# Staging x's seven units in PSUM at the joints of pairs, in a Strassen-type attention and mixture-of-experts kernel on one core

## The chip, the core and the metric

The kernel runs on one core of one Trainium2 chip. The metric is device time in microseconds. The engines are named as in the profile: PE (matmul), PEld (its weight loads), DVE (vector), ACT (scalar), POOL (GpSimd), SP (the queue that issues DMAs). Each engine works through its own instructions in program order, and engines wait for each other by semaphores.

## The reference

```python
# attention in chunks of 64 tokens: q, k, v are (8, 8, 576, 64)
scores = scale * np.matmul(q_c, k_c.transpose(0, 1, 2, 4, 3))
attn = np.exp(scores - max) / (sum + 1e-09)
out = np.matmul(attn, v_c)
# the result as x (4608, 512) goes through 4 experts, w1 (4, 512, 1024), w2 (4, 1024, 512)
p = domain_probs / (domain_probs.sum(-1, keepdims=True) + 1e-09)
for e in range(E):
    h = np.maximum(x @ w1[e], 0.0)
    out += p[:, e:e + 1] * (h @ w2[e])
```

## The kernel before

The 4608 tokens are nine blocks of 512. The first block is done plainly; the other eight are four pairs (0 to 3) of two blocks. For a pair the kernel makes eight passes, one for each half of each expert (passes 8 to 39 of the program), so the last passes of a pair that another one follows are 15, 23 and 31. The stretch from such a pass into the next is called a joint here; joints 1, 2 and 3 lie around 475 to 531, 796 to 852 and 1113 to 1169 us of the profile.

A pass multiplies matrices of 2 by 2 blocks with seven products instead of eight (Strassen's scheme). Every float32 operand is split into a high part (rounded to the type that PE multiplies, by a cast on ACT) and a low part (what the rounding left, a subtraction on DVE or POOL), and a product is six matmuls of 128x512, three for each of two blocks of rows. For x of a pair the seven units are `b11 b21 b22 t1 t2 t3 t4`; their parts lie in tiles `xh0..xh6` and `xl0..xl6`. They stay the same through the pair's eight passes and have to be made anew at a joint, while PE still works on the old ones.

The order of PE is written out in `WOVEN`, 28 steps to a pass: `g` and `h` are products of x with w1 (the two column groups), `a` and `b` are products of the pass before with w2.

```python
WOVEN = (
    "a1 g1 a2 g2 g6 a5 g5 a6 a3 g7 a7 g4 g3 a4 h1 h2 b1 b5 h6 b6 b3 h5 b7 h7 b2 b4 h4 h3".split()
)
```

Behind each step `later_pass` issues the work of the other engines that is listed for it in `at`; the number in `add(at, 13, ...)` is the step's place in `WOVEN` from 0. So a step's number sets the place of the work in each engine's order. `late` is the list that goes into the following pass. A step of that following pass is written with a stroke here: a1', g1', a2' are its first three.

The names in the profile's rows: `A`, `B`, `C` are PSUM banks of PE's sums. `s<-A` (L711, ACT) keeps the running sum of a product, and the next x product waits for it. `wraw<-A,s` or `wf<-C,ws` (L811, DVE) are the hidden values; `hf` are their high parts (L823, ACT) and low parts (L826, POOL); `wraw<-wf,wraw` (L817, DVE or POOL) are sums of hidden values. `acc<-A,acc` (L873, DVE) adds an output product to its sum, after which PE may write that bank again. L363 and L366 are the helpers that make a high and a low part. In pass 15 and 16 alone `wf<-v_in`, `wf<-e` and the like (L503 on ACT, L504 on POOL) also make the last factors of w2.

`psa` is one PSUM tile of two banks, `[128, 2, 512]`, in which the attention's scores live. In the last pass of a pair no attention runs, and there the kernel of before puts the unit t4 in it. `e` and `pt` are the attention's two SBUF tiles, which there hold the unit t2.

Of the kernel before, what the change touches and what calls it, by code (L numbers as in the profile page):

```python
# [12 lines left out]
ALU = mybir.AluOpType  # L13
# [18 lines left out]
def chunk_attention_moe(ctx: ExitStack, tc: tile.TileContext, qk, v, v0, dp, w1, w2, out):  # L32
# [10 lines left out]
    nc = tc.nc  # L43
# [72 lines left out]
    psa = ps_a.tile([P, 2, 2 * HG * C], F32, name="psa")  # L116

    def a_load(t):
        s = st[t] = {}
        s["x"] = load.tile([P, 2, 2, HG, C], F32, name="qk_in")  # L120
        nc.sync.dma_start(out=s["x"], in_=qk[t].rearrange("g c d x h s -> (c d) g x h s"))
# [240 lines left out]
    def hi_part(src, t):  # L362
        nc.scalar.copy(out=t[0], in_=src)  # L363

    def lo_part(eng, src, t):
        eng.tensor_tensor(out=t[1], in0=src, in1=t[0].bitcast(F32), op=ALU.subtract)  # L366
# [203 lines left out]
    xt = {}  # L570
# [11 lines left out]
    class Tokens:  # L582
# [26 lines left out]
            for k, t in enumerate(self.t2):  # L609
                eng.tensor_tensor(out=t, in0=self.b22[:, k], in1=self.t1[:, k], op=ALU.subtract)  # L610

        def sum4_apart(self):

            for k, t in enumerate(self.t2):
                nc.vector.tensor_tensor(out=psa[:, k], in0=self.b21[:, k], in1=t, op=ALU.subtract)
            self.t4 = psa

        def split2(self):
            i = self.KEYS["t2"]
            x_alloc(i)  # L620
            for k, t in enumerate(self.t2):
                hi_part(t, [part[:, k] for part in xt[i]])

        def lo2(self, k):
            lo_part(nc.vector, self.t2[k], [part[:, k] for part in xt[self.KEYS["t2"]]])

        def sum3(self, eng=None):
            self.less("t3", "b22", "b12", self.b12, eng)
# [220 lines left out]
    class Outer:  # L849
# [17 lines left out]
        def add(self, src, i, s):  # L867
            key = self.n // n_pass, 2 * i + self.g + NK * s
            if key not in acc:
                acc[key] = opool.tile([P, SUB], F32, name=f"acc{key[1]}")  # L870
                nc.scalar.copy(out=acc[key], in_=src)
            else:
                nc.vector.tensor_tensor(out=acc[key], in0=src, in1=acc[key], op=ALU.add)  # L873
# [493 lines left out]
    def probs_load(n, s):  # L1367
        e = n % n_pass // 2
        i = int(s == 0 and e % 2)
        if i:  # L1370
            pb[1:] = [hpool.tile([P, SUB], F32, name="s4")]
        elif not pb:
            pb.append(wpool.tile([P, PAIR, SUB], F32, name="ws"))
        t = pb[1] if i else pb[0][:, s]
        r = e * n_tiles + (1 + (n // n_pass - 1) * PAIR + s) * NT
        nc.sync.dma_start(
            out=t, in_=p_t[r : r + NT, :].rearrange("t p -> (t p)").partition_broadcast(P)
        )
# [14 lines left out]
    def first_load(pair):  # L1393
        if pair < n_pairs:
            a_load((1 + pair * PAIR) * NT)
# [69 lines left out]
    def half_sums(at, g, places, eng=None):  # L1465
        for i, name in zip(places, SUMS):
            if i is not None:
                add(at, i, lambda name=name: half_sum(g, name, eng))
# [3 lines left out]
    def later_pass(n, ahead, late, held):  # L1472

        first_pass, last_pass = n % n_pass == 0, n % n_pass == n_pass - 1
        pair, more = n // n_pass - 1, n + 1 < n_run
        at, first = {}, {}
        left, sc = Units(n), Scaled(n)
        steps = {"gh"[g]: LaterGroup(g, left, sc, False) for g in range(2)}
        steps |= {"ab"[g]: Outer(g, n - 1, ahead[1], ahead[0], False) for g in range(2)}

        def put(i, name, k, of=sc):
            add(at, i, lambda: of.hi(name, k), lambda: of.lo(name, k))

        for f in held:
            add(at, 0, f)
        second_half(at, ahead[0], *((9, False) if n == n_pass + 1 else ()))
        for i, f in late:
            add(at, i, f)

        add(at, 12, lambda: sc.sum("t3", 0, nc.gpsimd))  # L1490
        put(16, "b11", 0)
        put(16, "b11", 1)
        add(at, 18, lambda: sc.sum("t2", 0))
        put(19, "t2", 0)
        put(20, "b22", 0)
        add(at, 22, lambda: sc.sum("t1", 0))
        put(22, "t3", 0)
        put(23, "t1", 0)
        put(24, "b21", 0)
        put(24, "b22", 1)  # L1500
        put(26, "b21", 1)
        if more:
            add(at, 26, lambda: sc.sum("t4", 0, nc.gpsimd))
        add(at, 27, lambda: sc.sum("t1", 1), lambda: sc.sum("t3", 1))
        for i, f in later:
            add(at, i - len(WOVEN), f)
        later.clear()
        if n % 2 and more:
            add(at, 18, lambda: probs_load(n + 1, 0))
            add(at, 27, lambda: probs_load(n + 1, 1))  # L1510
        if pair + 1 < n_pairs:
            for places, i in TILES.get(n % n_pass, ()):
                attend(at, pair + 1, (16, 20, 23) if pair == 0 and places == LATE else places, i)
        late = []
        if n + 1 < 2 * n_pass - 1:
            add(at, 5, lambda: half_load(n + 1, 0))
            add(at, 13, lambda: half_load(n + 1, 1, (0,)))
            add(at, 19, lambda: half_load(n + 1, 1, (1,)))
            half_sums(at, 0, (12 if n % n_pass in (3, 5) else 15, 21, 21, 21))
        if n_pass < n < 2 * n_pass - 1:  # L1520
            half_sums(first, 1, (5, 6, 9, 10) if n == n_pass + 1 else (8, 8, 8, 12))
            if n == n_pass + 1:
                half_sums(first, 0, (None, None, None, 3))
            for i in (3, 10, 12, *MAKE_AT[3:]) if n == n_pass + 1 else MAKE_AT:
                add(first if i == 24 else at, i, lambda: make_next(0))
        for m, makes, raws in (
            (2 * n_pass - 1, (20, 26), ((8, load, "v_in"), (21, load, "v_in"), (22, att, "e"), (23, att, "pt"))),
            (2 * n_pass, (4, 9, 11, 14, 20), ((1, hpool, "s4"), (2, load, "v_in"), (13, hpool, "s4"))),
        ):
            if n == m:  # L1530
                for i in makes:
                    add(at, i, lambda: make_next(1))
                    add(at, i + 2, keep_made) if i + 2 < len(WOVEN) else later.append((i + 2, keep_made))
                for i, *place in raws:
                    add(at, i, lambda place=place: raw_load(*place))
        if n == 2 * n_pass - 1:
            add(at, 0, x_back)
        if first_pass and pair > 0:
            for i in range(4):
                for after, f in enumerate(outputs(pair - 1, 2 * (i // 2), i % 2)):  # L1540
                    add(at, 15 + 3 * i + after, f)
            apart = 4 if pair == 1 else 3
            late = [
                (1 + apart * i + after, f) for i in range(4)
                for after, f in enumerate(outputs(pair - 1, 1 + 2 * (i // 2), i % 2))
            ]
        if last_pass and more:
            xs = []

            def x(what, *args):  # L1550
                return lambda: getattr(xs[0], what)(*args)

            add(at, 5, lambda: xs.append(Tokens(pair + 1)), x("sum1"))
            add(at, 8, x("sum3", nc.gpsimd), x("sum2_apart", nc.gpsimd))
            add(at, 13, x("sum4_apart"))
            add(at, 15, x("hi", "b11"))
            add(at, 16, x("hi", "b21"), x("lo", "b11"))
            add(at, 18, x("lo", "b21"))
            add(at, 20, x("split2"), x("lo2", 0))
            add(at, 22 if pair == 0 else 20, x("lo2", 1))  # L1560
            add(at, 23, x("hi", "t1"))
            add(at, 25 if pair == 0 else 24, x("lo", "t1"))
            add(at, 25, x("hi", "t3"))
            add(at, 26, x("hi", "t4"))
            late = [
                (0, x("hi", "b22")), (0, lambda: first_load(pair + 2)), (5 if pair == 0 else 1, x("lo", "t3")),
                (6, x("lo", "t4")), (8, x("lo", "b22")),
            ]
        for i, name in enumerate(WOVEN):
            getattr(steps[name[0]], f"p{name[1]}")()  # L1570
            for f in first.get(i, []) + at.get(i, []):
                f()
        return (sc, left), late, ()

    def second_half(at, sc, t4=6, sum4=True):

        add(at, 0, lambda: sc.sum("t2", 1))
        add(at, 1, lambda: sc.hi("t1", 1), lambda: sc.lo("t1", 1))
        add(at, 3, lambda: sc.hi("t2", 1), lambda: sc.lo("t2", 1))
        add(at, 4, lambda: sc.hi("t3", 1), lambda: sc.lo("t3", 1))  # L1580
        if sum4:
            add(at, 4, lambda: sc.sum("t4", 1, nc.gpsimd))
        for k in range(2):
            add(at, t4 + k, lambda k=k: sc.hi("t4", k), lambda k=k: sc.lo("t4", k))
# [125 lines left out]
```

## Time and profile before

| what | us |
|---|---|
| three runs, median (lowest to highest) | 1485.78 (1485.12 to 1486.92) |
| span of the profiled execution, first to last instruction | 1484.2 |
| PE busy | 1467.3, 99% |
| PEld, DVE, POOL, ACT busy | 1201.5, 1086.1, 975.1, 625.3 (81, 73, 66, 42%) |

The profiled execution's own time is given as its span alone; the median of the runs is 1.6 us above it, which lies around the span. PE is busy all through: the other engines matter where PE has to wait for them. The clock that PE was granted is 0.998 of full speed, so its upper level, 2.4 GHz, all along.

### The profile page before, as it was taken

Reading aid. Unit: us, or ns where it says so; the run is one execution under the profiler, and the core shown is the slowest. Engines: PE = TensorE matmul, PEld = TensorE weight load, DVE = VectorE, ACT = ScalarE, POOL = GpSimd, SP = SyncE. Lnnn points to the kernel's source line nnn. Section 1 sums busy time; section 2 is a strip of 40 time slices with the busy share of each in tenths; the row PEclk is TensorE's granted clock in tenths of the full one; section 3 lists DMA queues with packets and bytes.
Section 4 is the critical chain, followed back from the end, with each engine's and each line's share of the span. In section 5 each row is a group of like instructions: output and inputs, shape, how many; then the busy total and the mean of one; then the engine's idle time right before and its main releaser. Section 6 shows DMA issues by size and latency. Waiting matters only on the chain.

```text
span 1484.2 us, 23314 instructions
## 1 busy us (share of the span) xinstructions
PE 1467.3 (99%) x8556; PEld 1201.5 (81%) x8556; DVE 1086.1 (73%) x1492; ACT 625.3 (42%) x1165; POOL 975.1 (66%) x728
## 2 busy tenths in 40 slices
PE   8999999999999999999999999999999999999998
PEld 7888887888888778888888888888888888888887
DVE  5566667899897876777776977777778866666665
ACT  4556534545453434334343434343433333333332
POOL 5778887888877785455557665545557655555555
PEclk9999999999999999999999999999999999999999
DMA  8799785878777679666665688666665696665655
GB/s 306 268 329 338 282 323 195 272 232 272 238 262 239 233 239 283 221 211 226 201 221 196 218 212 276 203 230 213 216 200 201 198 257 195 202 206 193 206 192 147
DMA packets 199074, 346.94 MB, mean 234 GB/s; under 512 B 70048, under 2 KB 110256, under 8 KB 198576
## 3 DMA queue, kind: packets, MB, share of 16 engines
q1 hardware_dynamic: 198960, 345.45, 71.0%
q8 instruction: 68, 1.11, 0.3%
q14 instruction: 46, 0.38, 0.1%
HBM read 274.01 MB, written 71.38 MB: 233 GB/s over the span
## 4 chain that ended last, share of the span: by engine, by line
PE 88%; POOL 5%; DMA 3%; DVE 2%; issue 1%; ACT 1%; SPq 1%; POOLq 0%; DVEq 0%; ACTq 0%
PE A L648 46%; PE C L648 26%; PE B L648 13%; POOL hf L826 2%; PE psa L208 1%; POOL wf L504 1%; PE psa L161 1%; DMA wf<-in_w 1%; POOL hf L366 1%; DMA v_in<-in_v 1%; POOL wraw L817 0%; DMA wf<-w 0%; DVE xl L366 0%; POOL wf L366 0%; DVE acc L873 0%
## 5 line engine op out<-in xcount | busy, mean ns | idle before, releaser
L826 POOL TENSOR_TENSOR hf<-wraw,hf 128x512 fp32r<-128x512 f32 x384 | 504.1, 1329 | 228.5 <-ACT hf L823 223.2
L648 PE MATMUL A<-hf,wf 128*128 128x512 f32 x1536 | 392.3, 391 | 0.3 <-POOL hf L826 0.2
L648 PE MATMUL A<-xh,wf 128*128 128x512 f32 (+1 forms) x1104 | 380.9, 388 | 1.2 <-DVE wraw L811 1.2
L823 ACT CAST hf<-wraw 128x512 fp32r<-128x512 f32 x384 | 234.4, 622 | 283.0 <-DVE wraw L817 88.5
L648 PEld LDWEIGHTS A<-hf,wf 128*128 128x128 f32 x1536 | 287.4, 188 | 63.4 <-DVE acc L873 3.1
L648 PEld LDWEIGHTS A<-xh,wf 128*128 128x128 f32 x1104 | 206.7, 188 | 44.5 <-DVE wraw L811 1.6
L711 ACT COPY s<-A 128x512 f32<-128x512 f32 x192 | 112.9, 588 | 305.7 <-PE A L648 305.6
L648 PE MATMUL A<-xl,wf 128*128 128x512 f32 (+1 forms) x552 | 213.7, 388 | 0.0
L648 PE MATMUL C<-xh,wf 128*128 128x512 f32 (+1 forms) x600 | 205.5, 390 | 3.0 <-POOL wf L504 2.2
L873 DVE TENSOR_TENSOR acc<-A,acc 128x512 f32<-128x512 f32 x232 | 158.0, 682 | 66.1 <-PE A L648 65.0
L648 PE MATMUL C<-hf,wf 128*128 128x512 f32 x768 | 195.6, 390 | 2.6 <-POOL wf L504 2.0
L648 PEld LDWEIGHTS C<-hf,wf 128*128 128x128 f32 x768 | 143.8, 188 | 33.8 <-POOL wf L504 2.4
L817 POOL TENSOR_TENSOR wf<-wraw,wf 128x512 f32<-128x512 f32 x31 | 40.6, 1310 | 150.2 <-DVE wf L811 150.2
L648 PEld LDWEIGHTS C<-xh,wf 128*128 128x128 f32 x600 | 111.5, 188 | 27.7 <-POOL wf L504 2.6
L648 PE MATMUL B<-xh,wf 128*128 128x512 f32 (+1 forms) x376 | 125.2, 384 | 0.0
L873 DVE TENSOR_TENSOR acc<-C,acc 128x512 f32<-128x512 f32 x120 | 82.7, 689 | 53.8 <-PE C L648 52.8
L648 PEld LDWEIGHTS A<-xl,wf 128*128 128x128 f32 x552 | 103.5, 188 | 21.1
L826 POOL TENSOR_TENSOR hf<-wf,hf 128x512 fp32r<-128x512 f32 x64 | 94.0, 1469 | 33.9 <-ACT hf L823 33.5
L648 PE MATMUL C<-xl,wf 128*128 128x512 f32 (+1 forms) x300 | 114.9, 386 | 0.0
L817 DVE TENSOR_TENSOR wraw<-wf,wraw 128x512 f32<-128x512 f32 x64 | 95.3, 1489 | 5.2 <-POOL hf L826 4.1
L648 PE MATMUL B<-hf,wf 128*128 128x512 f32 x384 | 98.4, 391 | 0.5 <-POOL hf L826 0.5
L817 POOL TENSOR_TENSOR wraw<-wraw 128x512 f32<-128x512 f32 x63 | 92.1, 1462 | 0.0
(199 smaller groups left out, 1957.2 us busy)
## 6 DMA issues: line engine op xcount, KB each, us to landing
wf<-w SPq DMA_DIRECT2D x399, 512.0 KB, 4.2
w<-wf SPq DMA_DIRECT2D x49, 512.0 KB, 5.1
qk_in<-in_qk SPq DMA_DIRECT2D x32, 512.0 KB, 5.0
w<-hf SPq DMA_DIRECT2D x28, 512.0 KB, 7.5
w<-hf SPq DMA_DIRECT2D x42, 256.0 KB, 5.5
wf<-in_w SPq DMA_DIRECT2D x19, 512.0 KB, 7.0
ws<-p_t SPq DMA_DIRECT2D x24, 256.0 KB, 3.9
xraw<-in_w SPq DMA_DIRECT2D x24, 256.0 KB, 5.2
```

The lines of the kernel that those rows point to most:

```text
L161: nc.tensor.matmul(s["sc"][of_half(half), c, slot], lhsT=q, rhs=k, start=True, stop=True)
L208: nc.tensor.matmul(av[of_half(slot % 2), half, head // 2], lhsT=s["v"][of_half(half), head], rhs=s["pt"][of_half(half), c, slot], start=Tr ...
L366: eng.tensor_tensor(out=t[1], in0=src, in1=t[0].bitcast(F32), op=ALU.subtract)
L504: nc.gpsimd.tensor_tensor(out=t[:, :, 1], in0=src, in1=t[:, :, 0].bitcast(F32), op=ALU.subtract)
L648: nc.tensor.matmul(out, lhsT=lhs(k, a), rhs=rhs(k, b), start=first and i == 0, stop=last and i == len(parts) - 1, skip_group_check=not (fi ...
L711: nc.scalar.copy(out=t, in_=self.a)
L817: (eng or nc.vector).tensor_tensor(out=self.values[place, k], in0=self.values[a, k], in1=self.values[b, k], op=op)
L823: nc.scalar.copy(out=self.part(name, 0)[:, k], in_=self.values[name, k])
L826: (eng or nc.gpsimd).tensor_tensor(out=self.part(name, 1)[:, k], in0=self.values[name, k], in1=self.part(name, 0)[:, k].bitcast(F32), op=A ...
L873: nc.vector.tensor_tensor(out=acc[key], in0=src, in1=acc[key], op=ALU.add)
```

## The change

Before, DVE took a unit's low part from where the unit lies in SBUF, in one subtraction of 128x1024 (two of 128x512 for t2). Now ACT first copies the unit, in two halves of 128x512, to `psa` (`stage`), and DVE subtracts from there, half by half (`lo_staged`). t4 is now computed in place in SBUF from the staged t2 (`sum4_staged`) instead of into `psa`; and the steps at which the parts are made are others.

```diff
-        def sum4_apart(self):
-
-            for k, t in enumerate(self.t2):
-                nc.vector.tensor_tensor(out=psa[:, k], in0=self.b21[:, k], in1=t, op=ALU.subtract)
-            self.t4 = psa
+        def stage(self, name):
+
+            of = getattr(self, name)
+            for k in range(2):
+                nc.scalar.copy(out=psa[:, k], in_=of[k] if name == "t2" else of[:, k])
+
+        def lo_staged(self, name):
+            for k in range(2):
+                lo_part(nc.vector, psa[:, k], [part[:, k] for part in xt[self.KEYS[name]]])
+
+        def sum4_staged(self):
+
+            for k in range(2):
+                nc.vector.tensor_tensor(
+                    out=self.b21[:, k], in0=self.b21[:, k], in1=psa[:, k], op=ALU.subtract
+                )
+            self.t4 = self.b21
...
-            add(at, 13, x("sum4_apart"))
-            add(at, 15, x("hi", "b11"))
-            add(at, 16, x("hi", "b21"), x("lo", "b11"))
-            add(at, 18, x("lo", "b21"))
-            add(at, 20, x("split2"), x("lo2", 0))
-            add(at, 22 if pair == 0 else 20, x("lo2", 1))
-            add(at, 23, x("hi", "t1"))
-            add(at, 25 if pair == 0 else 24, x("lo", "t1"))
-            add(at, 25, x("hi", "t3"))
-            add(at, 26, x("hi", "t4"))
+            add(at, 14, x("stage", "b11"))
+            add(at, 15, x("hi", "b11"), x("lo_staged", "b11"))
+            add(at, 16, x("hi", "b21"))
+            add(at, 17, x("stage", "b21"))
+            add(at, 18, x("lo_staged", "b21"))
+            add(at, 19, x("stage", "t2"))
+            add(at, 20, x("split2"), x("lo_staged", "t2"), x("sum4_staged"))
+            add(at, 22, x("stage", "t1"))
+            add(at, 23, x("hi", "t1"), x("lo_staged", "t1"))
+            add(at, 24, x("stage", "t3"))
+            add(at, 25, x("hi", "t3"), x("lo_staged", "t3"))
+            add(at, 26, x("hi", "t4"), x("stage", "t4"))
             late = [
-                (0, x("hi", "b22")), (0, lambda: first_load(pair + 2)), (5 if pair == 0 else 1, x("lo", "t3")),
-                (6, x("lo", "t4")), (8, x("lo", "b22")),
+                (0, x("hi", "b22")), (0, x("lo_staged", "t4")), (0, lambda: first_load(pair + 2)),
+                (1, x("stage", "b22")), (2, x("lo_staged", "b22")),
             ]
```

PE's, POOL's and SP's instructions stand in the same order as before. ACT's and DVE's do not. First ACT at joint 2, from the keeping of h6's sum (`s<-A`) to the cast of t3's high part; `xh_8339` of before and `xh_8365` of now are t2's high part, `qk_in` holds t1. Before:

```order
L711 COPY s_8312<-A_8255 128x512
L823 CAST hf_8326<-wraw 128x512
L823 CAST hf_8336<-wraw 128x512
L363 CAST xh_8339<-e 128x512
L363 CAST xh_8339<-pt 128x512
L823 CAST hf_8362<-wf_8243 128x512
L711 COPY s_8374<-A_8255 128x512
L823 CAST hf_8379<-wraw 128x512
L363 CAST xh_8382<-qk_in 128x1024
```

The same place now, where each stage waits for DVE to have read the unit before it out of `psa`:

```order
L616 COPY psa<-xraw 128x512 x2
L720 COPY s_8335<-A_8273 128x512
L832 CAST hf_8350<-wraw 128x512
L616 COPY psa<-e 128x512
L616 COPY psa<-pt 128x512
L832 CAST hf_8362<-wraw 128x512
L363 CAST xh_8365<-e 128x512
L363 CAST xh_8365<-pt 128x512
L832 CAST hf_8390<-wf_8263 128x512
L616 COPY psa<-qk_in 128x512 x2
L720 COPY s_8404<-A_8273 128x512
L832 CAST hf_8409<-wraw 128x512
```

Six copies have come in between; the keeping of h7's sum (`s_8404`) now stands behind t1's two copies.

DVE at joint 2, from the hidden values of h7 to those of h4 (`wraw<-A,s`), for which g1' waits. Before:

```order
L811 SCALAR_TENSOR_TENSOR wraw<-B_8373,ws 128x512
L873 TENSOR_TENSOR acc_6031<-B_8385,acc_6031 128x512
L366 TENSOR_TENSOR xl_8383<-qk_in,xh_8382 128x1024
L873 TENSOR_TENSOR acc_6193<-A_8279,acc_6193 128x512
L811 SCALAR_TENSOR_TENSOR wraw<-A_8255,s_7619 128x512
```

Now:

```order
L820 SCALAR_TENSOR_TENSOR wraw<-B_8403,ws 128x512
L366 TENSOR_TENSOR xl_8413<-psa,xh_8412 128x512 x2
L882 TENSOR_TENSOR acc_6051<-B_8417,acc_6051 128x512
L882 TENSOR_TENSOR acc_6213<-A_8301,acc_6213 128x512
L366 TENSOR_TENSOR xl_8442<-psa,xh_8441 128x512 x2
L820 SCALAR_TENSOR_TENSOR wraw<-A_8273,s_7639 128x512
```

The low part of t3 (`xl_8442`), which stood in the next pass, now stands ahead of the hidden values of h4.

DVE in the first steps of the pass behind joint 2, from the sum at a1' to the sum at a5' (`acc<-C`), for which a3' waits. Before:

```order
L873 TENSOR_TENSOR acc_5817<-A_8438,acc_5817 128x512
L817 TENSOR_TENSOR wraw<-wraw 128x512
L366 TENSOR_TENSOR xl_8409<-xraw,xh_8408 128x1024
L873 TENSOR_TENSOR acc_5817<-B_8464,acc_5817 128x512
L846 TENSOR_TENSOR B_8474<-B_8474,s_8459 128x512
L811 SCALAR_TENSOR_TENSOR wraw<-B_8474,ws 128x512
L873 TENSOR_TENSOR acc_5879<-C_8499,acc_5879 128x512
```

Now:

```order
L882 TENSOR_TENSOR acc_5837<-A_8475,acc_5837 128x512
L826 TENSOR_TENSOR wraw<-wraw 128x512
L366 TENSOR_TENSOR xl_8458<-psa,xh_8457 128x512 x2
L882 TENSOR_TENSOR acc_5837<-B_8504,acc_5837 128x512
L366 TENSOR_TENSOR xl_8485<-psa,xh_8484 128x512 x2
L855 TENSOR_TENSOR B_8516<-B_8516,s_8498 128x512
L820 SCALAR_TENSOR_TENSOR wraw<-B_8516,ws 128x512
L882 TENSOR_TENSOR acc_5899<-C_8541,acc_5899 128x512
```

Two low parts (t4, b22) stand ahead of that sum instead of one (t3), the second behind a stage of ACT.

## Rows read from the trace of the kernel before

**Rows 1.** The waits of PE over the whole span: who waited for whom, us in total, times, longest.

```profile
PE C L648 <- POOL wf L504: 4.2, 2, 2.2
...
PE A L648 <- DVE wraw L811: 1.2, 1, 1.2
```

**Rows 2.** Busy time of each engine at the three joints (us and instructions), the granted clock, the DMA engines' share and GB/s.

```profile
474.00:531.00 57.00, 53.32 (x232) 42.80 (x231) 49.13 (x56) 24.41 (x39) 46.36 (x33) 1.00 0.71 246
796.00:852.00 56.00, 56.00 (x247) 45.93 (x246) 50.16 (x60) 23.45 (x37) 41.78 (x29) 1.00 0.63 206
1113.00:1169.00 56.00, 56.00 (x247) 45.91 (x246) 50.18 (x60) 23.45 (x37) 41.87 (x29) 1.00 0.59 197
```

**Rows 3.** PE in order of time at joint 1: start, us, what, and in brackets the idle time before and what ended it. The first is g1', the second within a5', the third within a3'.

```profile
516.59 0.50 PE L648 MATMUL A<-xh,wf 128*128 128x512 f32 x1 [1.18 <-DVE wraw L811]
...
523.72 0.73 PE L648 MATMUL C<-hf,wf 128*128 128x512 f32 x2 [0.48 <-POOL hf L826]
...
529.66 1.20 PE L648 MATMUL C<-hf,wf 128*128 128x512 f32 x4 [2.02 <-POOL wf L504]
```

**Rows 4.** DVE in order of time at joint 1: t1's low part and the hidden values of h4.

```profile
513.62 2.31 DVE L366 TENSOR_TENSOR xl<-qk_in,xh 128x1024 fp32r<-128x1024 f32 x1
515.86 0.68 DVE L811 SCALAR_TENSOR_TENSOR wraw<-A,s 128x512 f32<-128x512 f32 x1
```

**Rows 5.** POOL in order of time at joint 1, beside these.

```profile
510.59 4.27 POOL L826 TENSOR_TENSOR hf<-wraw,hf 128x512 fp32r<-128x512 f32 x3
```

**Rows 6.** The low parts by their inputs (line L366, DVE): ns at least, median, at most; first and last start in us; shapes.

```profile
L366 DVE TENSOR_TENSOR xl<-xraw,xh x17: 1211/1651/2340, 179.3 to 1165.4; 128x1024 fp32r<-128x1024 f32 x17
...
L366 DVE TENSOR_TENSOR xl<-B,xh x3: 676/692/692, 13.3 to 29.2; 128x512 fp32r<-128x512 f32 x3
...
L366 DVE TENSOR_TENSOR xl<-psa,xh x3: 1212/1215/1215, 527.2 to 1162.8; 128x1024 fp32r<-128x1024 f32 x3
```

**Rows 7.** ACT's operations by form: count, busy us, mean ns of one, idle time before them. PSUM to SBUF, SBUF to SBUF, PSUM to PSUM, and the cast of a whole unit.

```profile
L823 ACT CAST hf<-wraw 128x512 fp32r<-128x512 f32 x384 | 234.4, 622 | 283.0 <-DVE wraw L817 88.5 <-POOL wraw L817 69.0 <-PE A L648 53.5
L711 ACT COPY s<-A 128x512 f32<-128x512 f32 x192 | 112.9, 588 | 305.7 <-PE A L648 305.6
...
L243 ACT ACTIVATE psa<-psa 128x512 f32<-128x512 f32 x33 | 19.3, 585 | 77.7 <-DVE psa L240 73.5 <-DVE xraw L491 4.0
L363 ACT CAST xh<-xraw 128x1024 fp32r<-128x1024 f32 x18 | 18.8, 1051 | 4.5 <-PE B L648 2.3 <-DVE xraw L595 2.2
```

**Rows 8.** ACT in order of time where the attention places its weights: L198 writes the tile that L194 wrote, and waits for it.

```profile
450.36 0.59 ACT L711 COPY s<-A 128x512 f32<-128x512 f32 x1 [1.69 <-PE A L648]
450.85 0.59 ACT L194 COPY pt<-psa 128x512 f32<-128x512 f32 x1
451.47 1.49 ACT L198 COPY pt<-psa 32x256 f32<-32x256 f32 x4
```

**Rows 9.** PE in order of time at joint 2: the last two matmuls of b6, the whole of b7, the last of h7, then b4, a1', the first matmul of g1', and a3'.

```profile
823.60 0.62 PE L648 MATMUL A<-hf,wf 128*128 128x512 f32 x2
...
826.77 1.65 PE L648 MATMUL A<-hf,wf 128*128 128x512 f32 x6
...
829.41 0.39 PE L648 MATMUL A<-xh,wf 128*128 128x512 f32 x1
...
831.00 1.52 PE L648 MATMUL A<-hf,wf 128*128 128x512 f32 x6
...
835.16 1.66 PE L648 MATMUL A<-hf,wf 128*128 128x512 f32 x6
836.65 0.39 PE L648 MATMUL A<-xh,wf 128*128 128x512 f32 x1
...
846.17 1.52 PE L648 MATMUL C<-hf,wf 128*128 128x512 f32 x6
```

**Rows 10.** DVE in order of time at joint 2.

```profile
823.21 1.77 DVE L817 TENSOR_TENSOR wraw<-wf,wraw 128x512 f32<-128x512 f32 x1 [0.58 <-POOL hf L826]
...
830.21 1.18 DVE L817 TENSOR_TENSOR wraw<-wraw 128x512 f32<-128x512 f32 x1
...
832.03 0.69 DVE L811 SCALAR_TENSOR_TENSOR wraw<-B,ws 128x512 f32<-128x512 f32 x1
...
834.42 0.68 DVE L873 TENSOR_TENSOR acc<-A,acc 128x512 f32<-128x512 f32 x1
835.03 0.68 DVE L811 SCALAR_TENSOR_TENSOR wraw<-A,s 128x512 f32<-128x512 f32 x1
...
845.10 0.68 DVE L873 TENSOR_TENSOR acc<-C,acc 128x512 f32<-128x512 f32 x1
```

**Rows 11.** ACT in order of time at joint 2: b21's high part, then the keeping of h7's sum, the cast of the hidden values' t1, and the high part of x's t1.

```profile
821.22 1.05 ACT L363 CAST xh<-xraw 128x1024 fp32r<-128x1024 f32 x1
...
829.90 0.59 ACT L711 COPY s<-A 128x512 f32<-128x512 f32 x1 [0.74 <-PE A L648]
831.42 0.62 ACT L823 CAST hf<-wraw 128x512 fp32r<-128x512 f32 x1 [0.94 <-DVE wraw L817]
831.94 1.04 ACT L363 CAST xh<-qk_in 128x1024 fp32r<-128x1024 f32 x1
```

**Rows 12.** POOL in order of time at joint 2.

```profile
820.87 3.56 POOL L826 TENSOR_TENSOR hf<-wraw,hf 128x512 fp32r<-128x512 f32 x2 [3.27 <-ACT hf L823]
...
832.12 1.30 POOL L826 TENSOR_TENSOR hf<-wraw,hf 128x512 fp32r<-128x512 f32 x1 [1.28 <-ACT hf L823]
```

More of the change, by code (lines that the diff above doesn't have):

```diff
@@ L622, in split2 @@
                 hi_part(t, [part[:, k] for part in xt[i]])
-        def lo2(self, k):
-            lo_part(nc.vector, self.t2[k], [part[:, k] for part in xt[self.KEYS["t2"]]])
         def sum3(self, eng=None):
```

## The prediction

> **What bounds the kernel now.** I read the busy times first: PE is busy for 99% of the span, so time can be won or lost only where PE waits. The view of PE's waits comes next [rows 1]: the longest are for POOL making factors (L504) and for DVE's hidden values (L811). Then the three joints by themselves [rows 2]: PE stands for 57.00 - 53.32 = 3.68 us at joint 1 and not at all at joints 2 and 3, where it is busy for 56.00 of 56.00 us. The clock is at its upper level in all three, so nothing is to be had there. The timeline of joint 1 says where the 3.68 us lie [rows 3]: 1.18 ahead of g1', 0.48 within a5', 2.02 within a3'.
>
> The first of them shows what the change is about. t1's low part took 2.31 us [rows 4], against 1.21 for the fastest of such [rows 6]. POOL's three operations beside it ended at 510.59 + 4.27 = 514.86 [rows 5], and the subtraction ended 1.07 later, at 515.93: it had stood until POOL was through. POOL is held in the same way: two operations take 3.56 us at joint 2 [rows 12] where one alone takes 1.30. When DVE has a PSUM input no such holding shows: from a bank the subtraction takes 676 to 692 ns, from `psa` 1212 to 1215 [rows 6].
>
> So the change can win at most 3.68 us, all at joint 1. What it can lose is open, as DVE and ACT stand right behind PE: at joint 2 DVE's `acc<-A` ends at 834.42 + 0.68 = 835.10 and a1' starts at 835.16; the hidden values of h4 end at 835.71, and g1' starts at 836.65 [rows 9, 10], a margin of 0.94.
>
> **What the change costs, in busy time.** A unit's low part becomes two subtractions of about 0.69 that start 0.60 apart, so about 1.29 from start to end against 1.21 unheld: nothing to speak of for DVE. ACT gets 14 copies more at a joint. None from SBUF to PSUM stands in the trace; the nearest rows are 622 ns SBUF to SBUF, 588 PSUM to SBUF and 585 PSUM to PSUM [rows 7], so I take 0.59. The second half writes the same tile as the first and waits for it. Such a wait costs 0.03: 450.85 + 0.59 = 451.44, and the next starts at 451.47 [rows 8]. A stage is then 2 x 0.59 + 0.03, about 1.22. Bounds: 1.07 if the halves overlap as 450.36 and 450.85 do (0.49 apart), 1.27 at 0.62 each. 7 x 1.22 is 8.5 us more of ACT, which is busy for 24 of 57 us there [rows 2]: no bound by itself.
>
> The Trainium skill's page "ScalarE: Activation LUTs", section "Step-by-step: what each stage is for", says that ScalarE writes PSUM faster than SBUF. In the rows the two differ by 3 ns (585 and 588), so by them nothing changes; were a copy 0.1 us shorter by that rule, each joint's loss below would be some 0.8 us less.
>
> **What it costs in order.** `psa` holds one unit. A stage may start only when DVE has read the unit before, and DVE may subtract only when stage and high part are done; both engines take their work in order, so each of these waits also holds what stands behind it. Joint 2 worked through, with the orders of ACT and DVE shown above. An operation's successor on its engine starts 0.08 to 0.10 before its end; hand-overs are 0.03 between ACT and DVE (831.39 to 831.42) [rows 10, 11] and 0.10 from PE to ACT (829.80 to 829.90) [rows 9, 11].
> - POOL's two operations at 820.87 are no longer held and end at 823.41 (1.25 + 1.29). DVE's sum behind them, now done at 823.21 + 1.77 = 824.98, is done 0.55 later, at 823.96 (the same 0.55 as now: 820.87 + 3.56 = 824.43). This is the gain, 1.0 us.
> - b21 has been staged by then (822.17 to 823.39). Its low part: 823.88 to 825.16.
> - ACT stages t2: 825.19 to 826.41, then casts a hidden value and t2's high part (0.52 + 0.52 + 0.62): 827.97. DVE: t2's low part from 827.48, t4 in place to 829.96. DVE's next sum ends at 830.56, and b4 needs it at 831.00: just in time.
> - ACT stages t1: 829.99 to 831.21. Behind it stand the keeping of h7's sum, a cast and t1's high part: 833.18 (before: 831.94 + 1.04 = 832.98, with nothing behind it waiting).
> - DVE: t1's low part 833.21 to 834.49, then two sums, the second done at 835.69. a1' starts at 835.74, not 835.16.
> - ACT stages t3: 834.52 to 835.74, its high part ends at 836.69. DVE: t3's low part 836.72 to 838.00, then the hidden values of h4, done at 838.60. g1' starts at 838.65 and not at 836.65: **2.0 us lost**.
>
> Behind that, DVE makes h3's hidden values (to 839.93) and three sums, the first two each held by POOL: 841.16 and 842.9. For the third, DVE is ready at 843.42, and POOL's next operation can start at 843.36, too near to call. If POOL is first the sum is done at 845.2, else at 844.0; call that S. Then come t4's low part (1.20), b22's stage, which waits for it (0.03 + 1.22), b22's low part (0.03 + 1.28), two operations on g2' (0.72 + 0.61 less the overlap of 0.08) and `acc<-C` (0.68): S + 5.7, where it is done at 845.10 + 0.68 = 845.78 now. a3' needs it. Unhindered, a3' would start seven products of 1.36 behind g1', at 848.2; it starts at 849.7 or 850.9 instead of 846.17 [rows 9]: 3.55 or 4.75 lost. I take the middle, **4.15 us**, and the same at joint 3, whose rows agree with joint 2's [rows 2].
>
> Joint 1 by the same walk: a cast more (L503) stands ahead of t2's high part and moves the chain by 0.52, so h4's hidden values end at 517.80 and g1' starts at 517.85 instead of 516.59. Then ACT's cast of the hidden values' t2 stands behind b22's stage and ends at 526.8; POOL's four operations from there (4 x 1.27, no longer held) end at 531.9, and the third matmul of a3' starts at 531.98, not 529.66 [rows 3]: **2.3 us lost** although POOL is free of DVE.
>
> The sum: 2.3 + 2 x 4.15 = 10.6 us. The median lies 1.6 above the span of the profiled execution (1485.78 and 1484.2); nothing there changes, so 1485.8 + 10.6 = **1496.4**. With stages of 1.07 instead of 1.22, four of which lie on each chain, it is 1.8 less (1494.6); with 1.27, 0.6 more. A dozen hand-overs and the two ties leave some 4 us to either side: the likeliest case by itself runs from 1490 to 1500.
>
> **Rivals.** *Relief (faster).* DVE and POOL no longer hold each other, the stalls of joint 1 go, and nothing new comes: 1485.8 - 3.7 = 1482.1. For it speaks every held row above; against it, that the same rows give 1.0 us at joint 2 and the chain takes 3.0. It decides if the hidden values of h4 are done by 836.6 at joint 2, that is if three stages cost some 2 us less than I say. The Trainium skill states the holding as a rule ("GPSIMD Engine Reference", section "Key points": its SBUF interfaces are shared with VectorE, with contention from instructions with two SBUF inputs), and rows 4 and 5 agree with it; the rule is silent on ACT, where I see the cost.
>
> *Absorbed (no change).* The margins (0.94 at g1') and the relief at joint 1 (up to 3.7) pay for most of it: a loss of 1 us at each of joints 2 and 3 and a gain of 1 to 2 at joint 1 come to about 1486. It needs a chain 1 us shorter at each joint and DVE first in the ties.
>
> **How the numbers follow.** 0.2% is 3 us, and about what a measurement of this kernel can tell from no change. Slower by the chain: 0.78. Absorbed: 0.11. Relief: 0.11, counted as faster by over 0.2%. The range from 1486.5 to 1500 leaves out relief, a small part of the second case (0.04) and the end of the first above 1500 (0.04).
>
> **What would show it.** Right: PE waits at joints 2 and 3, ahead of g1' for DVE's L820, some 1.5 to 2.5 us, and within a6' and a3' for ACT, POOL or DVE; ACT idle ahead of its stages (L616), ended by DVE's L366; POOL's operations there near 1.3 instead of up to 1.8; low parts from `psa` at 0.69. Wrong: copies to PSUM well below 0.5 or the halves running into each other; low parts that start before their stage's second half; or joints 2 and 3 without a wait of PE, whatever the total.

## The result and the profile after

The changed kernel takes **1500.07 us** (1499.63 to 1501.63), the kernel before 1486.24 (1485.12 to 1486.92) on the same chip: a ratio of 1.0095, 95% interval 1.0084 to 1.0107. That is 13.8 us slower; forecast were 10.6 us, and a range that ended at 1500.0. The profiled executions differ by 14.3 us of span.

First the page's busy times, then PE's waits (line, what was waited for, us in total, times, longest), which answer to [rows 1].

```profile
span 1498.5 us, 23364 instructions
...
PE 1473.2 (98%) x8556; PEld 1202.6 (80%) x8556; DVE 1074.9 (72%) x1510; ACT 647.5 (43%) x1207; POOL 964.0 (64%) x728
```

```profile
PE A L657 <- DVE wraw L820: 3.9, 3, 1.3
PE C L657 <- POOL wf L504: 3.8, 2, 2.2
PE A L657 <- DVE acc L882: 2.6, 4, 0.8
...
PE C L657 <- DVE acc L882: 1.9, 3, 0.7
PE A L657 <- POOL hf L835: 1.9, 3, 0.9
...
PE A L657 <- ACT hf L832: 0.7, 2, 0.4
```

DVE and POOL are busy for 11 us less each than before, and PE waits for them more: one wait for hidden values at every joint (L820, 3 of 1.3) where before only joint 1 had one, new waits for `acc` sums and for ACT's casts, and longer ones for POOL's low parts (1.9 in all on bank A, 0.2 before). So busy time was won and order was lost. PE at joint 2, in order of time, answers to [rows 9]: b4, a1', g1', two waits within a6', and a3'.

```profile
835.65 1.58 PE L657 MATMUL A<-hf,wf 128*128 128x512 f32 x6
...
840.71 1.65 PE L657 MATMUL A<-hf,wf 128*128 128x512 f32 x6 [0.75 <-DVE acc L882]
...
843.66 0.50 PE L657 MATMUL A<-xh,wf 128*128 128x512 f32 x1 [1.29 <-DVE wraw L820]
...
853.26 0.50 PE L657 MATMUL A<-hf,wf 128*128 128x512 f32 x1 [0.37 <-ACT hf L832]
...
854.62 0.72 PE L657 MATMUL A<-hf,wf 128*128 128x512 f32 x2 [0.86 <-POOL hf L835]
...
855.96 1.65 PE L657 MATMUL C<-hf,wf 128*128 128x512 f32 x6 [0.62 <-DVE acc L882]
```

Against the starts in [rows 9], b4 is 4.65 us late here (from joint 1), a1' 5.55, g1' 7.01 and a3' 9.79: joint 2 loses 5.1. At joint 3 the a3' is 14.65 late, by the starts of the same PE instructions in the two traces, so from one a3' to the next another 4.9 are lost. DVE's rows show what is late: the low parts of t1, t3, t4 and b22, and behind the last of them `acc<-C`.

```profile
838.17 1.29 DVE L366 TENSOR_TENSOR xl<-psa,xh 128x512 fp32r<-128x512 f32 x2
...
841.72 1.29 DVE L366 TENSOR_TENSOR xl<-psa,xh 128x512 fp32r<-128x512 f32 x2 [1.06 <-ACT xh L363]
842.92 0.68 DVE L820 SCALAR_TENSOR_TENSOR wraw<-A,s 128x512 f32<-128x512 f32 x1
...
848.41 1.80 DVE L826 TENSOR_TENSOR wraw<-wraw 128x512 f32<-128x512 f32 x1
850.13 1.27 DVE L366 TENSOR_TENSOR xl<-psa,xh 128x512 fp32r<-128x512 f32 x2
...
852.69 1.29 DVE L366 TENSOR_TENSOR xl<-psa,xh 128x512 fp32r<-128x512 f32 x2 [0.68 <-ACT psa L616]
...
855.23 0.68 DVE L882 TENSOR_TENSOR acc<-C,acc 128x512 f32<-128x512 f32 x1
```

Joint 1 answers to [rows 3]: PE's g1', then two matmuls of a3' and its third to sixth; below them a window table with PE's clock in the eighth place (window, its length and PE's busy time, PEld, DVE, ACT, POOL, PEclk, DMA share, GB/s).

```profile
517.72 0.50 PE L657 MATMUL A<-xh,wf 128*128 128x512 f32 x1 [1.30 <-DVE wraw L820]
...
529.49 0.70 PE L657 MATMUL C<-hf,wf 128*128 128x512 f32 x2 [0.68 <-DVE acc L882]
531.77 2.08 PE L657 MATMUL C<-hf,wf 128*128 128x512 f32 x4 [1.58 <-POOL wf L504]
```

```profile
475.00:531.00 56.00, 51.66 (x220) 40.32 (x218) 44.28 (x61) 31.47 (x53) 39.55 (x29) 1.00 0.72 238
531.00:533.00 2.00, 1.23 (x3) 1.05 (x4) 0.00 (x0) 0.14 (x1) 2.00 (x3) 0.50 0.30 123
533.00:538.00 5.00, 5.00 (x13) 3.90 (x13) 1.54 (x3) 1.56 (x3) 1.56 (x2) 0.54 0.17 69
538.00:541.00 3.00, 3.00 (x15) 2.44 (x14) 1.83 (x3) 0.06 (x1) 2.17 (x2) 1.00 0.13 15
```

The third matmul of a3' starts 2.11 us after its time in [rows 3]. Then PE runs at half clock (1.2 of 2.4 GHz): by the clock's records for 6.83 us from 530.8. The same matmul behind that stretch, first before and then now:

```profile
537.51 0.39 PE L648 MATMUL A<-xh,wf 128*128 128x512 f32 x1
```

```profile
542.35 0.39 PE L657 MATMUL A<-xh,wf 128*128 128x512 f32 x1
```

It is 4.84 late: 2.7 us that no wait shows. Up to b4 of joint 2 PE wins 0.2 of the 4.84 back. As PE was 0.35 early when joint 1 began, the waits of joint 1 are 2.46 from there.

### The profile page after: what moved, and what is told of

It reads as the page before. It is cut to its first block, busy times and chain, and to the rows that moved or that the text cites. A ratio compares the mean times of both kernels' runs of the same rounds, so it can differ in the third digit from the quotient of the medians.

```text
span 1498.5 us, 23364 instructions
## 1 busy us (share of the span) xinstructions
PE 1473.2 (98%) x8556; PEld 1202.6 (80%) x8556; DVE 1074.9 (72%) x1510; ACT 647.5 (43%) x1207; POOL 964.0 (64%) x728
## 4 chain that ended last, share of the span: by engine, by line
PE 84%; DVE 5%; POOL 4%; ACT 3%; DMA 2%; issue 1%; SPq 0%; POOLq 0%; DVEq 0%; ACTq 0%
PE A L657 44%; PE C L657 24%; PE B L657 12%; POOL hf L835 2%; DVE xl L366 1%; PE psa L208 1%; PE psa L161 1%; POOL hf L366 1%; POOL wf L504 1%; DMA w<-hf 1%; ACT psa L616 1%; DMA wf<-in_w 1%; ACT xh L363 1%; DVE wraw L826 0%; DVE wf L826 0%
## 5 line engine op out<-in xcount | busy, mean ns | idle before, releaser
L835 POOL TENSOR_TENSOR hf<-wraw,hf 128x512 fp32r<-128x512 f32 x384 | 496.2, 1308 | 252.0 <-ACT hf L832 249.0
```

The lines of the kernel that those rows point to most:

```text
L835: (eng or nc.gpsimd).tensor_tensor(out=self.part(name, 1)[:, k], in0=self.values[name, k], in1=self.part(name, 0)[:, k].bitcast(F32), op=A ...
```

## The experiments

Two theories stood at first. **Copies:** the stages and the one `psa` pair they go through make the loss. **Order:** the low parts now stand too early in DVE's queue, wherever they read from. Medians below stand beside 1485.7 to 1486.0 for the kernel before, run with each batch.

**x1: the order of the changed kernel without the copies**, low parts and t4 from SBUF, in halves.

```diff
 def stage(self, name):
-    for k in range(2):
-        nc.scalar.copy(out=psa[:, k], in_=...)
+    return
 def lo_staged(self, name):
-        lo_part(nc.vector, psa[:, k], ...)
+        lo_part(nc.vector, src, ...)
```

> The changed kernel with its steps as they stand, but without the copies: stage() does nothing, the low parts (still in halves) and t4 read the unit in SBUF. Theory (the chain of copy and subtraction through the one psa pair makes the loss): ACT is free, DVE waits for high parts alone; t3's low part still stands ahead of h4's hidden values and is held by POOL (1.3 to 2.2 us against a margin of 0.94), so PE waits up to 1.3 us ahead of g1' at joints 2 and 3 and little else: 1486 to 1490 us. Rival 1 (the new order of DVE alone makes the loss): 1498 to 1501 us. Rival 2 (DVE and POOL holding each other is worse than the copies): above 1500.

Measured: 1508.19 us (1507.34 to 1508.93), ratio 1.0148 [1.0131, 1.0165]. Without the copies it is 8.1 us slower still. Both profiles have as much half clock at the joints, x1's 3.41 us at joint 1 and as much at joint 2. DVE at joint 2 says why: t1's low part, then b22's, and `acc<-C` behind it.

```profile
841.14 2.66 DVE L366 TENSOR_TENSOR xl<-qk_in,xh 128x512 fp32r<-128x512 f32 x2 [0.30 <-ACT xh L363]
...
854.51 2.88 DVE L366 TENSOR_TENSOR xl<-xraw,xh 128x512 fp32r<-128x512 f32 x2
...
858.64 0.68 DVE L882 TENSOR_TENSOR acc<-C,acc 128x512 f32<-128x512 f32 x1
```

2.66 and 2.88 stand against 1.29 from `psa`; t3's and t4's low parts, between them, took 1.28 from SBUF too. So the theory that copies and pair alone make the loss fell: the order loses without any copy, and staging pays part of it back. The order here includes t4's difference, which now stands at step 20 and not at 13; x12 comes back to it.

**x2: all seven units staged, but t3, t4 and b22 in the following pass.**

```diff
-add(at, 24, x("stage", "t3"))
-add(at, 25, x("hi", "t3"), x("lo_staged", "t3"))
-add(at, 26, x("hi", "t4"), x("stage", "t4"))
+add(at, 25, x("hi", "t3"))
+add(at, 26, x("hi", "t4"))
 late = [
-    (0, x("hi", "b22")), (0, x("lo_staged", "t4")), ...
-    (1, x("stage", "b22")), (2, x("lo_staged", "b22")),
+    (0, x("hi", "b22")), ...
+    (1, x("stage", "t3")), (3, x("lo_staged", "t3")),
+    (4, x("stage", "t4")), (6, x("lo_staged", "t4")),
+    (6, x("stage", "b22")), (8, x("lo_staged", "b22")),
```

> The changed kernel with all seven units staged, but t3, t4 and b22 staged and subtracted in the following pass, at its steps 1 and 3, 4 and 6, 6 and 8. Theory: g1' no longer waits for t3's chain (1.3 us at joints 2 and 3) and a6', a3' not for t4's and b22's (about 1.9 us); what is left is the wait of a1' for t1's chain (0.75): 1486 to 1490 us. Rival (14 copies more on ACT cost by themselves, wherever they stand): 1495 or more.

Measured: 1485.12 us (1484.07 to 1485.86), ratio 0.9993 [0.9984, 1.0003], a little under the expectation. With as many copies through the same pair, the whole loss is gone. What remains at joints 2 and 3 is 0.75 ahead of a1', for `acc`; at joint 1 PE is 1.7 us faster than before, by the starts of the same PE instructions. The edit moves three stages on ACT together with three subtractions on DVE, so it does not part the two queues.

**x3: a unit copied and subtracted in one piece of 128x1024**, t2 apart (it lies in two tiles).

```diff
-for k in range(2):
-    nc.scalar.copy(out=psa[:, k], in_=of[:, k])
+nc.scalar.copy(out=psa, in_=of)
...
-for k in range(2):
-    lo_part(nc.vector, psa[:, k], [part[:, k] for part in xt[self.KEYS[name]]])
+lo_part(nc.vector, psa, xt[self.KEYS[name]])
```

> The changed kernel with each unit but t2 copied in one piece of 128x1024 and subtracted in one piece. Theory: a stage takes 1.05 instead of 1.22 and a subtraction 1.21 instead of 1.29; three or four such links lie on each chain, so some 0.8 to 1.0 us less at each joint, and 2.7 more at joint 1 if the slow clock there does not come: 1494 to 1498 us. Rival (the order alone): unchanged at 1500.

Measured: 1496.26 us (1495.22 to 1496.88), ratio 1.0065 [1.005, 1.008], as expected. The wait for hidden values ahead of g1' is 1.0 instead of 1.3, and the profile has no lower clock at joint 1, although a3' there waits 0.62 and 1.65, no less than in the changed kernel.

**x4: staging at joint 1 alone**, the other joints as before.

```diff
+if pair == 0:
     add(at, 14, x("stage", "b11"))
     ...
+else:
+    add(at, 13, x("sum4_apart"))
+    ...
```

> Staging at joint 1 alone; joints 2 and 3 as before the change. Theory: the loss of joint 1 as in the changed kernel's trace, 2.4 us in waits and 2.7 in the slow clock behind them, 5.1 in all: 1491.0 us, with the granted clock at half for some 7 us behind a3'; without that stretch 1488.5. Rival (the joints hang together, so that one alone costs nothing): 1486.

Measured: 1489.61 us (1486.62 to 1492.71 in eight executions), ratio 1.0017 [1.0006, 1.0029]. There are two levels: three executions at 1486.6 to 1486.8 with a mean granted clock of 0.999, five at 1489.6 to 1492.7 with 0.994 to 0.998. That is between the two totals expected, 1491.0 and 1488.5. The profiled execution is of the second kind; at the waits within a3' it has 6.83 us at half clock, and joint 1 costs it 2.4 us of waits and 2.7 behind them, as expected. It is lower than 1491.0 because PE was already 1.0 us early ahead of the joint. So the mean clock is lower in some executions than in others, by some 3 us; that it is joint 1 where it falls is seen in the profiled one alone.

**x6 and x7: which units' place makes which wait.** x6 takes t3's low part from SBUF in the following pass, where the kernel before has it; x7 does so with t4 and b22.

```diff
 x6
-add(at, 24, x("stage", "t3"))
-add(at, 25, x("hi", "t3"), x("lo_staged", "t3"))
+add(at, 25, x("hi", "t3"))
 late = [ ...
+    (5 if pair == 0 else 1, x("lo", "t3")),
 x7
-add(at, 26, x("hi", "t4"), x("stage", "t4"))
+add(at, 26, x("hi", "t4"))
 late = [ ...
-    (0, x("lo_staged", "t4")), (1, x("stage", "b22")), (2, x("lo_staged", "b22")),
+    (6, x("lo", "t4")), (8, x("lo", "b22")),
```

> The changed kernel, with t3's low part alone put back: it is taken from SBUF in the following pass, after the step where the kernel before has it; t4 and b22 stay staged and early. Theory A (one queue: all of DVE's work ahead of acc<-C sets a3', wherever in that stretch it stands): the 1.29 us wait ahead of g1' goes at joints 2 and 3, and the wait within a3' grows by about as much, so the total stays at 1498 to 1502. Theory B (each wait of PE counts by itself): the 1.29 us at joints 2 and 3 are won, and at joint 1 the 1.3 us: 1495 to 1497.

> The changed kernel, with the low parts of t4 and b22 put back: taken from SBUF in the following pass, at the steps where the kernel before has them; b11, b21, t2, t1 and t3 stay staged. Both theories: the waits ahead of a1' (0.75) and g1' (1.29) stay at joints 2 and 3, those within a6' and a3' go: some 2.0 us a joint, and 1.6 at joint 1, so 1485.8 + 5.7, about 1491.5 (1490 to 1493; up to 2.7 more if the clock falls at joint 1 as it did in the changed kernel). If the loss at a3' were made by the copies on ScalarE rather than by the place of these two low parts, it would stay above 1495.

Measured: x6 1497.52 us (1495.67 to 1498.4), ratio 1.0076 [1.0062, 1.009]; x7 1492.11 us (1490.48 to 1492.86), ratio 1.004 [1.0026, 1.0054], as expected. PE's waits, x6 and then x7:

```profile
PE C L657 <- POOL wf L504: 4.7, 2, 2.6
PE C L657 <- DVE acc L882: 2.6, 3, 1.0
PE A L657 <- DVE acc L882: 2.6, 4, 0.8
PE A L657 <- POOL hf L835: 1.8, 3, 0.8
```

```profile
PE C L657 <- POOL wf L504: 4.2, 2, 2.2
PE A L657 <- DVE wraw L820: 3.9, 3, 1.3
PE A L657 <- DVE acc L882: 2.6, 4, 0.8
```

In x6 the three waits ahead of g1' (L820) are gone, in x7 those ahead of a3' for `acc<-C` and within a6' for POOL's low parts; neither removes the other's. By the starts of the same PE instructions, from b4 to a3', joint 2 loses 3.2 us in x6, 2.5 in x7, 5.1 in the changed kernel: t3's part is worth some 2.0, that of t4 and b22 some 2.6. Both edits take away stages as well as move subtractions. x6's total lies between its two theories: the waits went as theory B says, but its profile has 3.41 us at half clock at joint 2 and as much at joint 3, some 1.6 us of delay each, where the changed kernel has none.

**x10: joints 2 and 3 as in the changed kernel, joint 1 as before**, by the same edit with `pair != 0` for `pair == 0`.

> Joints 2 and 3 as in the changed kernel, joint 1 as in the kernel before. Theory (the joints add up, and joint 1's share is 2.4 us of waits and 2.7 us of lower clock): 1485.8 + 2 x 5.0 = 1495.9, with the clock at its upper level at all three joints. By the sum of the prediction joints 2 and 3 are worth 2 x 4.15, so 1494.1. Rival (the clock falls behind any of these late waits): a lower clock at joint 2 or 3 as well, 1.7 to 2.7 more each, 1498 to 1501.

Measured: 1497.49 us (1497.19 to 1497.74), ratio 1.0073 [1.0058, 1.0088]: above the theory, just below the rival. The waits come out as the theory has them (5.0 us at joint 2 and 4.9 at joint 3, before the clock), and a lower clock stands at joint 3, for 3.41 us. It costs 1.6 us by the starts of PE's instructions, and 1495.9 + 1.6 is the time measured. PE there, and two windows:

```profile
1171.81 0.73 PE L666 MATMUL A<-hf,wf 128*128 128x512 f32 x2 [0.85 <-POOL hf L844]
1173.16 2.58 PE L666 MATMUL C<-hf,wf 128*128 128x512 f32 x6 [0.62 <-DVE acc L891]
```

```profile
1168.00:1173.00 5.00, 3.32 (x13) 1.87 (x11) 4.29 (x8) 3.25 (x6) 2.52 (x3) 1.00 0.48 158
1173.00:1178.00 5.00, 4.84 (x14) 3.86 (x15) 1.39 (x3) 0.82 (x2) 3.71 (x3) 0.66 0.36 108
```

The six matmuls of a3' take 2.58 us here and 1.65 at joint 2 of the changed kernel, after the same waits (0.86 and 0.62 there).

**x8, x9, x11: what the idea is worth where nothing waits for it.** x8 has x2's late staging at joint 1 alone, by x4's edit. x9 is x2 with t1's low part behind `acc<-A` and h4's hidden values. x11 is x9 with units copied and subtracted whole, by x3's edit.

```diff
 x9, against x2
-add(at, 23, x("hi", "t1"), x("lo_staged", "t1"))
+add(at, 23, x("hi", "t1"))
+add(at, 26, x("lo_staged", "t1"))
```

> Joint 1 as in the kernel with the late staging (t3, t4 and b22 staged and subtracted in the following pass), joints 2 and 3 as in the kernel before. Theory: the relief of joint 1 alone remains (there the late staging gained 1.4 us of the 3.7 that PE stands, and joints 2 and 3 lost 0.75 each): 1484.0 to 1484.6, faster than the kernel before by some 0.1%. Rival: the gain at joint 1 was bought by what stands at joints 2 and 3, or is spent behind it: 1485.4 to 1486.4.

> The late staging at all three joints, and t1's low part moved behind acc<-A and h4's hidden values. Theory: the waits ahead of a1' at joints 2 and 3 (0.75 us each) go as well, and nothing takes their place: 1483.3 to 1484.3. Rival: the subtraction now stands ahead of h5's hidden values and POOL's factors, whose product waits instead: 1485 to 1486.

> The late staging with t1's low part behind h4's hidden values, and every unit but t2 copied and subtracted in one piece of 128x1024 instead of two halves: fewer instructions and fewer hand-overs, but a subtraction can't start on the first half. With the order relaxed nothing waits for the pair any more, so both theories: the same as with halves, within 1 us (1482 to 1484); if the hand-overs between halves still cost something at a joint, 1481 to 1482.

Measured: x8 1483.39 us (1482.27 to 1485.37), ratio 0.9983 [0.9974, 0.9992]; x9 1483.02 (1480.99 to 1485.7), 0.9982 [0.9973, 0.9992]; x11 1481.75 (1480.97 to 1482.34), 0.9968 [0.9955, 0.998]. All three beat both kernels, x11 by 4.2 us in its batch. x9's `acc` wait ahead of a1' is gone, as the theory has it. x8 and x9 gain a little more than expected; x11 lies where hand-overs between halves were to cost something, but x9 and x11 are not told apart: their intervals overlap. By the starts of the same PE instructions, joint 1 gives 1.7 us in x8's profile, 2.3 in x9's and 2.8 in x11's. PE's waits in x9:

```profile
PE C L657 <- POOL wf L504: 2.8, 2, 2.2
PE B L1038 <- DVE e L253: 2.1, 2, 1.9
PE C L1102 <- DVE s L1096: 1.2, 1, 1.2
```

**x12: x9's order without the copies**, low parts and t4 from SBUF by x1's edit: is it the order that wins, or the staging in it?

> The late staging with t1's low part behind h4's hidden values, in the same order on DVE, but nothing is staged: every low part and t4's difference are taken from SBUF, halves as they were. It tells whether the relaxed order wins, or the staging in it. Theory (staging wins: DVE and POOL hold each other again without it): 1485 to 1489. Rival (the order wins, the copies to the pair are worth nothing once the order is relaxed): 1482 to 1484.

Measured: 1497.58 us (1494.16 to 1498.05), ratio 1.0072 [1.0058, 1.0085], well above both. In this order the copies are worth 14.6 us (1497.58 against 1483.02); 2.8 of them are a lower clock at joint 1, which x12's profile has and x9's has not. But x12 is also 11.8 us slower than the kernel before, which has no copies either and makes the low parts of t3, t4 and b22 in the following pass too. One difference is t4's: at joint 2 its subtraction reads two SBUF tiles at step 20, and b4 waits for the `acc<-A` behind it. Another is the halves: t3's and t4's low parts took 2.42 and 2.85 there.

```profile
834.05 1.77 DVE L625 TENSOR_TENSOR xraw<-xraw,e 128x512 f32<-128x512 f32 x1
...
836.35 0.68 DVE L882 TENSOR_TENSOR acc<-A,acc 128x512 f32<-128x512 f32 x1
```

```profile
837.09 1.65 PE L657 MATMUL A<-hf,wf 128*128 128x512 f32 x6 [1.25 <-DVE acc L882]
```

So 14.6 is what the copies are worth with t4's difference and the halves where x9 has them; against the kernel before, x9 wins 2.8. The low parts by form (count, busy us, mean ns of one, idle before), x12 and then x9:

```profile
L366 DVE TENSOR_TENSOR xl<-xraw,xh 128x512 fp32r<-128x512 f32 x30 | 28.5, 988 | 0.0
...
L366 DVE TENSOR_TENSOR xl<-qk_in,xh 128x512 fp32r<-128x512 f32 x6 | 7.9, 1358 | 0.0
...
L366 DVE TENSOR_TENSOR xl<-e,xh 128x512 fp32r<-128x512 f32 x3 | 4.1, 1380 | 1.0 <-ACT xh L363 1.0
```

```profile
L366 DVE TENSOR_TENSOR xl<-psa,xh 128x512 fp32r<-128x512 f32 x42 | 26.9, 682 | 5.8 <-ACT xh L363 3.7 <-ACT psa L616 2.0
```

## Why the prediction was right in direction and too small

**Right: prices and walk.** A stage was put at two copies of 0.59 and one start to end of 1.22; a low part at 1.29:

```profile
L616 ACT COPY psa<-xraw 128x512 f32<-128x512 f32 x30 | 17.7, 589 | 9.7 <-DVE xl L366 9.2
```

```profile
834.94 1.21 ACT L616 COPY psa<-qk_in 128x512 f32<-128x512 f32 x2 [1.14 <-DVE xraw L625]
...
839.50 1.21 ACT L616 COPY psa<-xraw 128x512 f32<-128x512 f32 x2 [0.32 <-DVE xl L366]
```

The rule of the Trainium skill ("ScalarE: Activation LUTs", section "Step-by-step: what each stage is for") that ScalarE writes PSUM faster than SBUF shows little here: with a PSUM input, 585 ns for an ACTIVATE into PSUM stand against 588 for a copy into SBUF [rows 7]. With an SBUF input, a copy into PSUM took 589, and into SBUF only a cast to another type is there to compare, 622. The chain of stage, subtraction, stage came as walked: taken from POOL's two operations (at 825.66 now and at 820.87 before, so 4.79 later), a1' was due at 840.53 and started at 840.71, g1' was due at 843.44 and started at 843.66. From the third sum on, S + 5.7 was given for `acc<-C`: 848.41 + 1.80 = 850.21, and it ended at 855.23 + 0.68 = 855.91. The waits stood where they were named, and POOL was held less: the two operations took 2.55 us, not 3.56 [rows 12], though a sum of hidden values at 845.59 still took 1.75. Joint 1's waits came to 2.46, against 2.3.

```profile
825.66 2.55 POOL L835 TENSOR_TENSOR hf<-wraw,hf 128x512 fp32r<-128x512 f32 x2 [3.27 <-ACT hf L832]
...
848.37 1.29 POOL L835 TENSOR_TENSOR hf<-wraw,hf 128x512 fp32r<-128x512 f32 x1 [1.04 <-ACT hf L832]
```

**Wrong: the tie at joints 2 and 3.** The step "too near to call" took the middle of S = 844.0 and 845.2. POOL was first by 0.04 (848.37 against 848.41), and DVE's sum took 1.80. The later S gives 4.75 a joint, not 4.15: 2 x 0.6 = 1.2 us. What is left, 0.1 to 0.35 a joint (5.1 and 4.9 measured), are small delays along the chain. The tie alone would make the sum 1497.6, inside the range.

**Wrong: the clock.** The first step says that the clock is at its upper level at all joints, "so nothing is to be had there". It held for the kernel before, even after the 2.02 us wait of [rows 3]; that a change which adds waits may lose the level was put at nothing in the sum and in the range, and this took the time out of the range. In the profiled execution it cost 2.7 us at joint 1: 2.1 + 2.7 - 0.2 + 5.1 + 4.9 = 14.6, near the 14.3 of the spans. Nor was the clock up all along before the change, as the section on the time before says: behind the mean of 0.998 lie 3.41 us at half clock from 248.2 us, in the stage ahead of the joints, and the last 3.8 us of the span.

**What the rivals were worth.** *Absorbed* fell: no margin was left. *Relief* fell as a forecast, but its mechanism is the larger one. Staging saves 8.1 us in the changed kernel's order (x1) and 14.6 in x9's (x12), with t4's difference at step 20 in both; the prediction saw 1.0 at joint 2, since it compared only with the order before. There DVE's low parts also come from SBUF, but in whole units (t2 apart), and t4's difference stands at step 13, where PE at joint 2 waits for none of them; which of these counts for how much was not taken apart. The new order puts three units' low parts, with their stages, ahead of h4's hidden values and `acc<-C`, and this costs more than staging returns (x2, x6, x7). The Trainium skill's rule on SBUF interfaces shared by GpSimd and VectorE ("GPSIMD Engine Reference", section "Key points") agrees: 988 and 1358 ns with two SBUF inputs, 682 with one in PSUM.

**Open.** What decides whether the clock falls after these waits. Equal waits left it up at joint 2 of the changed kernel and not at joint 3 of x10, and x4 has executions of both kinds. Whether ACT's queue or DVE's alone would make the loss was not parted either, as x2, x6 and x7 move stages and subtractions together; x1 shows only that the order on DVE, without a stage, loses too. The clock does not explain the gains of x8 and x9: in their batch, executions with a mean granted clock of 0.998 have medians of 1485.6 us for the kernel before (nine of them), 1483.2 for x8 (six) and 1483.0 for x9 (four). In x8's profile some 1.3 us are clock, as the 3.41 us at half clock from about 248 us, which the profiles of the kernel before and of x9 have, are not there.

## What to carry to other kernels

A change that relieves an engine and moves work earlier has two prices: try the relief near the old places first, as x2 does. List what stands behind each moved operation in its engine's queue and leave it behind whatever PE waits for next; the seven staged units cost 14 us or win some 3 (x9), by the place of four units' subtractions and three of their stages. Where a walk ends in a tie, carry both ends to the sum, and where it adds waits to PE, allow for the clock too.

## What the runs showed that was not expected

PE's clock fell to half for 3.41 or 6.83 us at a time at waits ahead of or within a3', in some kernels and joints and not in others; in x4 the executions have two levels some 3 us apart, and the mean granted clock is lower at the slower one. And one copy of 128x1024 from SBUF to PSUM took 1016 ns (x11), 0.2 us less than two halves with their hand-over.
